# Identity built first on GpSimd, a 112-column last output piece, and newly searched orders and engines in a linear-attention and GEGLU block

## The chip, the cores and the metric

The kernel runs on one core of a Trainium2 chip, in one launch. The metric is device time in microseconds (us); the time before is the median of three runs, 190.91 us. TensorE is PE, its weight load PEld, VectorE DVE, ScalarE ACT, GpSimd POOL, and SyncE, which issues all DMAs, SP.

## The reference

```python
x = A_x                                   # [1, 2048, 448] bf16
h = x + _A_ref(_layernorm(x), A_wqkv, A_wo)
h2 = h + _B_ref(_layernorm(h), B_w_gate, B_w_up, B_w_down)

def _A_ref(x, wqkv, wo):                  # 16 heads of 28, no softmax
    q, k, v = split(x @ wqkv)             # wqkv [448, 1344]
    phi = lambda t: jnp.where(t > 0, t + 1, jnp.exp(t)) + 1e-6
    kv = einsum("bhsd,bhse->bhde", phi(k), v)
    z = einsum("bhsd->bhd", phi(k))
    num = einsum("bhqd,bhde->bhqe", phi(q), kv)
    den = einsum("bhqd,bhd->bhq", phi(q), z)[..., None] + 1e-6
    return merge_heads(num / den) @ wo    # wo [448, 448]

def _B_ref(x, w_gate, w_up, w_down):      # 448 -> 1792 -> 448
    return (gelu_tanh(x @ w_gate) * (x @ w_up)) @ w_down
```

## The kernel before

The 2048 rows are 16 tiles of 128 rows, numbered 0 to 15. Every piece of work is a named task with its engine, and the order in which each engine's tasks stand is a table of numbers in the source (`ORDERS`, five strings in the order PE, ACT, DVE, POOL, SP). A second table (`BANKS`) gives each PSUM tile one of the eight banks, and `ENGINE` names the engine of tasks that could run on more than one. Nothing is reordered when the kernel runs: an engine works through its string and waits on semaphores.

The tasks that the text speaks of, t being a tile:

- `warm` is ten matmuls of 512 columns on a tile of ones, whose result nobody reads; `ident` is the 128x128 identity, which POOL makes from the ones (L384).
- Layer norm 1: `ast`, `aag` on DVE (mean and variance, L423, L424), `aln`, `ars` on ACT (the root, by logarithm and exponential), `anm` (the negated mean), `norm` (L467 on DVE or L470 on POOL), `dup` (a copy of the last 64 columns, for odd tiles).
- `tr0` to `tr3` transpose tiles 0 to 3 on PE against the identity (L482 to L484) and `ev0` to `ev3` evict them; tiles from 4 on are transposed in pairs by a DMA, `xT5`, `xT7` and so on (L491).
- `ks0`, `ks1` are the k projections of the first two tiles (L524); `ka`, `kb` (L537) and `qa`, `qb` (L635) are the two halves of the k or q projection of a pair of tiles, `ka4` that of tiles 4 and 5. After k come `ek`, `cl`, `ph` (exponential, clamp, sum), after q `eq`, `cq`, `pq`.
- `g0a`, `g0b`, `g2a`, `g2b` with a tile's number add phi(k) times the normalised x into four PSUM banks (L561), four matmuls per tile in each of two groups of banks. Each such task is two matmuls that run side by side, one on the upper and one on the lower 64 rows of the array; `a` and `b` of one tile write the same two banks with the halves exchanged. The same holds for `ka`/`kb` and the other a/b pairs.
- Then `evg`, `zbm`, `evz`, `kvp`, `kz1`, `mm` fold v and wo into one matrix; `mul`, `den`, `rd`, `om`, `wo` divide by the denominator, project and add; layer norm 2 gives `hn` and its transposed tiles.
- `gua`/`gub` are the gate and up projections (L835, L838), `ge` the gelu on ACT (L861), `hm` the product on DVE (L863), `da`/`db` the down projection of a pair of tiles (L785), `down14`, `down15` those of the last two tiles alone (L799), `out` the residual sum on DVE (L805), `dout` the store (L807). The last tile is computed and stored in two pieces of columns.

All DMAs stand in the one queue of SP, in the order of its string.

```python
for t in self.order[ename]:            # emit(): one engine's string
    ...                                # waits on what t reads and overwrites
    ins = t.fn(eng)
```

Of the kernel before, what the change touches and what calls it, by code (L numbers as in the profile page):

```python
# [238 lines left out]
def bass_sequential_preLN__linear_attn_block__glu_gated_geglu__prompt_kernel(  # L239
# [34 lines left out]
    with es:  # L274
# [495 lines left out]
        p_op = []  # L770

        def b2_tile(t, kd):
            parts = [(0, D)] if t < T - 1 else [(0, D // 2), (D // 2, D)]
            pair = t < T - 2
            if pair and t % 2 == 0:
                p_op.clear()
# [162 lines left out]
```

## Time and profile before

| what | before |
|---|---|
| runs | 190.91, 190.93, 190.7 us |
| the profiled execution | 190.84 us, of which the span from first to last instruction is 189.1 us |
| granted PE clock | 1.000 |
| PE busy | 184.3 us (97%), 1940 matmuls |
| DVE, ACT, POOL busy | 117.3, 76.3, 69.1 us |

The profiled execution is 0.07 us under the median. Busy time of PE counts a matmul from its start to its modelled end; matmuls overlap, so the spacing of their starts tells the pace, and "mean ns of one" is longer than that spacing. In the timeline a row is a run of equal instructions: start, length to the end of the last, count, and in brackets the idle time before with what ended it.

### The profile page before, as it was taken

The page shows a single profiled execution, that of the slowest core. Times are in us where ns is not written, and L with a number is a line of the kernel's source. Part 1 is how long each engine was busy: PE and PEld are TensorE (multiplying, and loading weights), DVE is VectorE, ACT ScalarE, POOL GpSimd, SP SyncE. Part 2 cuts the span into 40 slices and gives each one's busy share as a digit, 9 for nine tenths or more (in the row PEclk, how much of TensorE's full clock was granted, in tenths as well). Part 3 has the DMA queues.
Part 4 walks back from the last instruction along what each step waited for, and adds up shares of the span by engine and source line. Part 5 has one row for each costly group of instructions (what it writes and reads, how often), then busy time and mean ns, then how long its engine had stood idle before and what let it go on. Part 6 is the DMA issues. An engine that isn't in the chain of part 4 may idle for free.

```text
span 189.1 us, 4840 instructions
## 1 busy us (share of the span) xinstructions
PE 184.3 (97%) x1940; PEld 105.8 (56%) x1940; DVE 117.3 (62%) x296; ACT 76.3 (40%) x210; POOL 69.1 (37%) x120
## 2 busy tenths in 40 slices
PE   7899999999999999999999999999999999999994
PEld 2344555544687886654444455445555666665643
DVE  7999966597998979368773438445534253344332
ACT  3789734688973432300343520043453223032200
POOL 1668732398889579910039500054000000000000
DMA  5898389806925372560003262002320000000204
GB/s 140 246 234 142 75 171 322 234 3 143 296 54 59 57 231 37 100 85 1 0 0 62 39 109 54 3 2 52 92 45 0 3 2 24 3 0 0 76 21 149
DMA packets 32694, 15.93 MB, mean 84 GB/s; under 512 B 21536, under 2 KB 32416, under 8 KB 32672
## 3 DMA queue, kind: packets, MB, share of 16 engines
q1 hardware_dynamic: 32672, 15.63, 36.1%
q8 instruction: 15, 0.25, 0.6%
q14 instruction: 7, 0.06, 0.1%
HBM read 8.37 MB, written 1.84 MB: 54 GB/s over the span
## 4 chain that ended last, share of the span: by engine, by line
PE 95%; DMA 1%; POOL 1%; DVE 1%; ACT 1%; issue 0%; POOLq 0%; DVEq 0%
PE ps L835 41%; PE ps L785 20%; PE ps L561 7%; PE ps L635 5%; PE ps L537 5%; PE ps L717 5%; PE ps L838 4%; PE ps L799 3%; DMA x_sb<-in_A_x_dram 1%; PE ps L524 1%; PE ps L706 1%; PE ps L618 1%; POOL xn L470 1%; PE ps L599 1%; DVE st L423 0%
## 5 line engine op out<-in xcount | busy, mean ns | idle before, releaser
L838 PE MATMUL ps<-hnT,wgu_sb 64*128 64x512 bf16 (+1 forms) x490 | 87.1, 333 | 0.0
L835 PE MATMUL ps<-hnT,wgu_sb 64*128 64x512 bf16 (+1 forms) x490 | 87.1, 333 | 0.0
L863 DVE TENSOR_TENSOR hh<-ps,gl 128x256 bf16<-128x256 f32 x112 | 42.5, 417 | 46.4 <-ACT gl L861 45.6
L861 ACT ACTIVATE gl<-ps 128x256 bf16<-128x256 f32 x112 | 36.0, 385 | 80.7 <-PE ps L838 38.7
L835 PEld LDWEIGHTS ps<-hnT,wgu_sb 64*128 64x128 bf16 x490 | 46.1, 94 | 32.4 <-issue 0.2
L838 PEld LDWEIGHTS ps<-hnT,wgu_sb 64*128 64x128 bf16 x490 | 45.9, 94 | 0.2
L785 PE MATMUL ps<-wd_sb,hh 64*128 64x448 bf16 x392 | 39.4, 349 | 0.0
L785 PEld LDWEIGHTS ps<-wd_sb,hh 64*128 64x128 bf16 x392 | 21.2, 94 | 15.8 <-issue 0.2
L680 POOL TENSOR_TENSOR o<-pq,rd 128x448 bf16<-128x448 bf16 x16 | 14.8, 943 | 20.4 <-DVE rd L677 20.4
L423 DVE BATCH_NORM_STATS2 st<-x_sb 128x6 f32<-128x448 bf16 x32 | 19.1, 613 | 0.5 <-DMA x_sb<-in_A_x_dram 0.4
L674 POOL TENSOR_TENSOR prod<-pq,zb 128x448 f32<-128x448 bf16 x16 | 16.3, 1034 | 4.2 <-DVE zb L270 4.2
L805 DVE TENSOR_TENSOR x_sb<-ps,x_sb 128x448 bf16<-128x448 f32 (+1 forms) x17 | 9.9, 590 | 8.9 <-PE ps L799 4.7
L561 PE MATMUL ps<-pk,xn 64*128 64x448 bf16 (+1 forms) x128 | 15.0, 350 | 0.1
L726 DVE TENSOR_TENSOR x_sb<-ps,x_sb 128x448 bf16<-128x448 f32 x16 | 9.4, 617 | 5.9 <-PE ps L717 5.0
L505 ACT ACTIVATE e<-ps 128x448 bf16<-128x448 f32 x20 | 10.1, 538 | 6.2 <-PE ps L537 5.4
L635 PE MATMUL ps<-wq_sb,xnT 64*128 64x448 bf16 x112 | 12.1, 350 | 0.0
L537 PE MATMUL ps<-wk_sb,xnT 64*128 64x448 bf16 x98 | 11.9, 350 | 0.2
L507 POOL TENSOR_SCALAR tm<-e 128x448 bf16<-128x448 bf16 x15 | 8.4, 563 | 8.3 <-ACT e L505 5.9
L429 POOL TENSOR_SCALAR nm<-mv 128x2 f32<-128x2 f32 (+1 forms) x13 | 2.9, 225 | 21.5 <-DVE mv L424 21.1
L717 PE MATMUL ps<-m_sb,oT 64*128 64x448 bf16 x98 | 10.7, 349 | 0.0
L512 DVE SCALAR_TENSOR_TENSOR pk<-ps,tm 128x448 bf16<-128x448 f32 x16 | 9.7, 619 | 1.0 <-ACT tm L503 0.3
L561 PEld LDWEIGHTS ps<-pk,xn 64*128 64x128 bf16 (+1 forms) x128 | 6.5, 97 | 6.6 <-PE ps L561 1.9
(84 smaller groups left out, 147.9 us busy)
## 6 DMA issues: line engine op xcount, KB each, us to landing
out_dram<-x_sb SPq DMA_DIRECT2D x15, 112.0 KB, 1.8
wd_sb<-in_B_w_down_dram SPq DMA_DIRECT2D x3, 448.0 KB, 6.5
wgu_sb<-in_B_w_up_dram SPq DMA_DIRECT2D x3, 384.0 KB, 6.9
wgu_sb<-in_B_w_gate_dram SPq DMA_DIRECT2D x3, 384.0 KB, 4.5
x_sb<-in_A_x_dram SPq DMA_DIRECT2D x2, 448.0 KB, 4.7
x_sb<-in_A_x_dram SPq DMA_DIRECT2D x4, 112.0 KB, 2.1
x_sb<-in_A_x_dram SPq DMA_DIRECT2D x2, 224.0 KB, 3.5
wo_sb<-in_A_wo_dram SPq DMA_DIRECT2D x1, 392.0 KB, 7.0
```

The lines of the kernel that those rows point to most:

```text
L423: op("dve", lambda e: e.bn_stats(st[:, t, :], src_ap()), [b_src], [b_st[t]], nm + "st%d" % t, 0.615, key)
L537: ins = e.matmul(ps[:, p_k[n].bank, 0:D], xnT[rows, t0 + n, k, :], wk_sb[rows, k, :], start=(k == 0 and not second), stop=(second and k == ...
L561: ins = e.matmul(ps[0:b - a, p_gx[cc].bank, 0:D], xnv(t, a, b)[rows], pk[rows, i, :], start=(t == 0 and not second), stop=(t == T - 1), sk ...
L635: ins = e.matmul(ps[:, p_q[n].bank, 0:D], xnT[rows, ts[n], k, :], wq_sb[rows, k, :], start=(k == 0 and not second), stop=(second and k == ...
L674: op(me, lambda e, ip=ip, p3=p3: e.tensor_tensor(prod[:, ip, :, 0:28], p3(), zb[:].rearrange("p (a e) -> p a e", e=28), ALU.mult), [b_pq[t ...
L680: return e.tensor_tensor(o2[:, so, n, :].rearrange("p (a e) -> p a e", e=28), p3(), rd[:, i, :].unsqueeze(2).to_broadcast([128, 16, 28]), ...
L717: ins = e.matmul(ps[:, p_h[n].bank, 0:D], oT2[rows, so, kk, :], m_sb[rows, kk, :], start=(k == 0 and not second), stop=(second and k == 2) ...
L785: ins = e.matmul(ps[:, p_d[n].bank, 0:D], hh[rows, j, u * 128:(u + 1) * 128], wd_sb[rows, j, :], start=(j == 0 and not second), stop=(j == ...
L835: e.matmul(ps[:, pa.bank, jj * N:(jj + 1) * N], wgu_sb[A_, wa + k if k < 3 else 3, jc], hnT[A_, k, c0:c0 + N], start=(k == 0 and jj == 0 a ...
L838: ins = e.matmul(ps[:, pb.bank, jj * N:(jj + 1) * N], wgu_sb[B_, wb + k if k < 3 else 3, jc], hnT[B_, k, c0:c0 + N], start=(k == 0 and jj ...
L861: G.add("act", lambda e, gi=gi, cs=cs, p_g=p_g: e.activation(gl[:, gi, cs], ps[:, p_g.bank, cs], AF.Gelu_apprx_tanh), r=[p_g], w=[b_gl[gi] ...
L863: op("dve", lambda e, dst=dst, gi=gi, cs=cs, p_u=p_u, rs_=rs_: e.tensor_tensor(dst, rs_(ps[:, p_u.bank, cs]), rs_(gl[:, gi, cs]), ALU.mult ...
```

## The change

The change replaces all of `ORDERS` and `BANKS` and the list `ENGINE`, and makes two edits in the code: the last tile's two pieces are 336 and 112 columns wide instead of 224 and 224, and a duration that only the planner reads is now a formula. All lines below the tables have moved down by one.

```diff
 ENGINE = (
-    "ev0:act anm1:act dup1:act dup3:pool norm4:dve dup5:pool dup9:pool cl2:act cl3:dve cl4:act cl5:act norm14:dve"
-    " norm15:dve dup15:pool cl7:act cl8:dve cl10:dve cl13:dve cl14:dve evz:dve evm1:act cq2:act cq4:act cq5:act cq6:act"
-    " cq7:act cq8:act cq13:act cq15:act evo1:dve evh0:dve evh1:act bnm2:act wrap3:pool wrap4:pool wrap5:pool wrap7:pool"
+    "anm0:act ev0:act ev1:act dup3:pool anm6:act dup7:pool anm8:act cl0:dve anm10:act cl2:act cl3:dve anm12:act cl4:act"
+    " norm15:dve dup15:dve cl6:dve cl7:act cl8:dve cl11:act cl13:dve cl14:dve evg0:act evg1:dve evm1:act cq4:act cq5:act"
+    " cq7:act cq8:act cq15:act evo1:dve evh0:dve evh1:act bnm2:act wrap2:pool bnm4:act wrap4:pool wrap5:pool wrap7:pool"
+    " bnm10:act bnm12:act"
 )
...
         def b2_tile(t, kd):
-            parts = [(0, D)] if t < T - 1 else [(0, D // 2), (D // 2, D)]
+            parts = [(0, D)] if t < T - 1 else [(0, 336), (336, D)]
...
-                   "out%d_%d" % (t, c0), 0.625 if c1 - c0 == D else 0.392, kd)
+                   "out%d_%d" % (t, c0), 0.16 + (c1 - c0) / 960.0, kd)
```

Of the order table the first entries of POOL show the manner of it (task numbers are those of the order in which the tasks are declared; 9 is `ones`, 10 `ident`, 11 `eps`, 46 `anm2`, 49 `norm2`):

```diff
-    "9 11 46 12 49 10 54 57 65 69 70 96 24 100 76 25 80 79 281 278 87 58 91 92 90 289 114 118 117 145 141 177 22 144 26 172"
+    "9 10 11 12 24 22 25 46 49 23 54 57 65 69 68 100 80 81 79 279 282 287 91 90 58 26 290 154 118 117 145 144 168 171 197"
```

The start of POOL's string before: `ones`, `eps`, `anm2`, `lnc`, `norm2`, `ident`, `anm3`, `norm3`.

```order
L383 MEMSET ones_bf 128x128
L386 MEMSET small 128x1
L429 ISA
L429 TENSOR_SCALAR nm<-mv 128x1
L387 MEMSET small 128x1
L470 TENSOR_SCALAR xn<-x_sb,nm,rs 128x448
L384 AFFINE_SELECT ident<-ones_bf 128x128
L429 TENSOR_SCALAR nm<-mv 128x1
L470 TENSOR_SCALAR xn<-x_sb,nm,rs 128x448
```

The same place now: `ones`, `ident`, four small constants, `mask_a`, `anm2`, `norm2`, then `powwarm` (L399), `anm3`, `norm3`.

```order
L384 MEMSET ones_bf 128x128
L385 ISA
L385 AFFINE_SELECT ident<-ones_bf 128x128
L387 MEMSET small 128x1
L388 MEMSET small 128x1
L400 MEMSET mones 112x4
L398 MEMSET small 128x2
L401 AFFINE_SELECT mtmp<-mones 112x4
L430 TENSOR_SCALAR nm<-mv 128x1
L471 TENSOR_SCALAR xn<-x_sb,nm,rs 128x448
L399 TENSOR_TENSOR small<-small 128x1
L430 TENSOR_SCALAR nm<-mv 128x1
```

The identity moved from behind `norm2` to the second place, and with it the ISA row (POOL's configuration, which the built program puts ahead of the first instruction that needs it); the one-element power that warms POOL (`powwarm`, before at L398 between later tasks) now stands between `norm2` and `anm3`. The first transposes on PE are `tr2`, `tr0`, `tr3`, `tr1` before and `tr2`, `tr0`, `tr1`, `tr3` now.

PE from `ks0` to the first matmuls of the g group before. The rows are `ks0` `ks1`; `ka2` `kb2`; `qa0` `qa2` `qb0` `qb2`; `ka4`; `g0a0`; `kb4`; and then `g0b0`, `g0a1`, `g0b1`, `g0a2` and the first matmul of `g2a0` in one row.

```order
L524 MATMUL ps<-wk_sb,xnT 128x448 x8
L537 MATMUL ps<-wk_sb,xnT 128x448 x14
L635 MATMUL ps<-wq_sb,xnT 128x448 x28
L537 MATMUL ps<-wk_sb,xnT 128x448 x8
L561 MATMUL ps<-pk,xn 128x448 x2
L537 MATMUL ps<-wk_sb,xnT 128x448 x6
L561 MATMUL ps<-pk,xn 128x448 x9
```

The same place now: `g0a0` and `g0b0` stand among the q halves (`qa0`; `g0a0`; `qb0` `qa2`; `g0b0`; `qb2`), then `ka4`, `g0a1`, `kb4`, `g0b1` and on.

```order
L525 MATMUL ps<-wk_sb,xnT 128x448 x8
L538 MATMUL ps<-wk_sb,xnT 128x448 x14
L636 MATMUL ps<-wq_sb,xnT 128x448 x8
L562 MATMUL ps<-pk,xn 128x448 x2
L636 MATMUL ps<-wq_sb,xnT 128x448 x14
L562 MATMUL ps<-pk,xn 128x448 x2
L636 MATMUL ps<-wq_sb,xnT 128x448 x6
L538 MATMUL ps<-wk_sb,xnT 128x448 x8
L562 MATMUL ps<-pk,xn 128x448 x2
L538 MATMUL ps<-wk_sb,xnT 128x448 x6
L562 MATMUL ps<-pk,xn 128x448 x3
```

Four matmuls moved ahead of `ka4`, and `kb4` now stands between `g0a1` and `g0b1`, which stood next to each other.

PE behind the single matmul `zbm` (L588) before: `g0b14`, `g0a15`, `g0b15` in one row, then `qa4`, `kvp`.

```order
L588 MATMUL ps<-gx,ones_bf 128x448
L561 MATMUL ps<-pk,xn 128x448 x6
L635 MATMUL ps<-wq_sb,xnT 128x448 x8
L599 MATMUL ps<-gx,wvt_sb 112x112 x4
L599 MATMUL ps<-gx,wv_sb 112x112 x12
```

The same place now: `g0b14`, `g0a15`; `qa4`; `g0b15`; `qb4`; `kvp`.

```order
L589 MATMUL ps<-gx,ones_bf 128x448
L562 MATMUL ps<-pk,xn 128x448 x4
L636 MATMUL ps<-wq_sb,xnT 128x448 x8
L562 MATMUL ps<-pk,xn 128x448 x2
L636 MATMUL ps<-wq_sb,xnT 128x448 x6
L600 MATMUL ps<-gx,wvt_sb 112x112 x4
L600 MATMUL ps<-gx,wv_sb 112x112 x12
```

`qa4` moved between `g0a15` and `g0b15`. In the rest of the program the gate, up and down tasks stand in another order too, without a new kind of row; at the end PE's last rows are 28 matmuls of `db12`, 14 of `down14` and 14 of the last piece in both.

75 rows, old and new, of tables (BANKS, ORDERS) are left out of this document.

## The prediction

> **What bounds the kernel now.** I read the page first, then busy time by stage, then PE's timeline where PE was not full. From the page:
>
> ```profile
> span 189.1 us, 4840 instructions
> PE 184.3 (97%) x1940; PEld 105.8 (56%) x1940; DVE 117.3 (62%) x296; ACT 76.3 (40%) x210; POOL 69.1 (37%) x120
> PE 95%; DMA 1%; POOL 1%; DVE 1%; ACT 1%; issue 0%; POOLq 0%; DVEq 0%
> ```
>
> PE is busy 97% of the span and makes up 95% of the chain that ended last. The stages (PE's busy time beside each stretch):
>
> ```profile
> 13.90:35.70 21.80, 21.73 (x223) 1.00 0.84 195
> 49.60:186.40 136.80, 136.80 (x1514) 1.00 0.24 50
> ```
>
> From 13.9 us on PE hardly pauses. A new order can win only ahead of 13.9, in short stalls inside the busy stretch, and after the last matmul; everywhere else it can only lose. PE's head:
>
> ```profile
> 5.53 0.34 PE L482 MATMUL ps<-ident,xn 128*128 128x128 bf16 x3 [0.86 <-POOL ident L384]
> 6.07 0.34 PE L482 MATMUL ps<-ident,xn 128*128 128x128 bf16 x3
> 6.65 0.34 PE L482 MATMUL ps<-ident,xn 128*128 128x128 bf16 x3
> 7.10 0.34 PE L482 MATMUL ps<-ident,xn 128*128 128x128 bf16 x3
> 7.56 2.00 PE L524 MATMUL ps<-wk_sb,xnT 128*128 128x448 bf16 x8
> 10.96 2.81 PE L635 MATMUL ps<-wq_sb,xnT 64*128 64x448 bf16 x28
> 13.91 0.93 PE L537 MATMUL ps<-wk_sb,xnT 64*128 64x448 bf16 x8
> ```
>
> These are tr2, tr0, tr3, tr1, ks0/ks1, the four q halves and ka4. One matmul of 448 columns lasts 0.35 and the next pair starts 0.19 later, so after the q halves (end 13.77) PE could have gone on at 13.77 - 0.35 + 0.19 = 13.61; ka4 came at 13.91: 0.30 idle.
>
> **The change, part by part.**
>
> *Identity first.* POOL's head, then DVE's, then ACT's row with ars1:
>
> ```profile
> 3.84 0.24 POOL L429 TENSOR_SCALAR nm<-mv 128x1 f32<-128x1 f32 x1 [2.81 <-DVE mv L424]
> 4.51 0.71 POOL L470 TENSOR_SCALAR xn<-x_sb,nm,rs 128x448 bf16<-128x448 bf16 x1 [0.40 <-ACT rs L436]
> 5.18 0.29 POOL L384 TENSOR_SCALAR_AFFINE_SELECT ident<-ones_bf 128x128 bf16<-128x128 bf16 x1
> 8.32 0.71 POOL L470 TENSOR_SCALAR xn<-x_sb,nm,rs 128x448 bf16<-128x448 bf16 x1 [0.41 <-ACT rs L436]
> 2.27 0.33 DVE L393 MEMSET xn<- 128x320 bf16 x1
> 5.64 0.36 DVE L467 TENSOR_SCALAR xn<-x_sb,mv,rs 128x448 bf16<-128x448 bf16 x1
> 5.92 0.62 DVE L423 BATCH_NORM_STATS2 st<-x_sb 128x6 f32<-128x448 bf16 x1
> 6.46 0.38 DVE L467 TENSOR_SCALAR xn<-x_sb,mv,rs 128x448 bf16<-128x448 bf16 x1
> 9.11 0.38 DVE L467 TENSOR_SCALAR xn<-x_sb,mv,rs 128x448 bf16<-128x448 bf16 x1
> 6.09 0.20 ACT L436 ACTIVATE rs<-ln 128x1 f32<-128x1 f32 x1
> ```
>
> The identity fits into POOL's 2.81 us of waiting, so tr2 waits for norm2 (4.51 + 0.71 = 5.22) and starts near 5.27, 0.26 earlier. Little of that lasts. tr0 hangs on norm0 (DVE 5.64), which comes about 0.09 earlier because its root now stands ahead of tile 3's: tr0 at 5.99. tr1 no longer stands behind tr3: norm1 comes at 6.4 (ars1 ends 6.29), tr1 at 6.81. But tile 3 loses: powwarm stands ahead of anm3 on POOL, and ars3 behind aln1 on ACT (about 6.14), so norm3 runs about 6.29 to 7.0. tr3 follows tr1 after 0.46 (6.65 to 7.10 gives 0.45) at 7.27, and ks0 comes 0.46 later at 7.73, where it was 7.56: **+0.17**. powwarm itself costs
>
> ```profile
> L398 POOL TENSOR_TENSOR small<-small x1: 575/575/575, 47.9 to 47.9; 128x1 f32<-128x1 f32 x1
> ```
>
> 0.58, which norm3 can bear up to tr1's end, 7.27.
>
> *g0a0 and g0b0 ahead of ka4.* Two pairs of matmuls, 2 x 0.19 = 0.38, go into the idle 0.30 and push ka4 to 13.61 + 0.17 + 0.38 = 14.16. Before, the same work would have been done at 13.91 + 0.38 = 14.29: **-0.13**, if ka4's data are there. They come by xT5:
>
> ```profile
> 9.52 1.33 SPq L491 DMA_TRANSPOSE xnT<-xn  x1
> DMA to landing us min/median/max: 2.8/3.1/4.6
> ```
>
> norm4 moved from DVE (9.11) to POOL behind norm5 (8.32, and 0.3 later now, because the memset of xn, 0.33, has moved from DVE's waiting time into its busy time ahead of aag4). So norm5 8.6 to 9.3, norm4 to 10.0, and xT5 is issued near 10.0 instead of 9.52. On SP's queue it still stands behind the x tiles 8 to 11 and ahead of 12 to 15. Before, it landed just ahead of 13.91, some 4.3 after its issue. With the same latency it is 0.5 later: ka4 at 14.4, work-equal +0.11. If the 448 KB transfer ahead of it sets the landing, nothing changes. Bounds -0.13 to +0.11; I take **-0.10**, nearer the first, since 4.3 against a median of 3.1 speaks for a wait behind that transfer. After ka4 the waits are close but covered: ph4, xT7 and ph6 come within 0.2 us of their use by the same reckoning.
>
> *Halves pulled apart.* g0b1 right behind g0a1, and g0b15 right behind g0a15, show a stall:
>
> ```profile
> 15.48 0.97 PE L561 MATMUL ps<-pk,xn 64*128 64x448 bf16 x6
> 35.58 0.98 PE L561 MATMUL ps<-pk,xn 64*128 64x448 bf16 x6
> 30.27 1.30 PE L561 MATMUL ps<-pk,xn 64*128 64x448 bf16 x12
> PEld ps L561 <- PE ps L561: 1.9, 5, 0.5
> ```
>
> Three pairs should take 2 x 0.19 + 0.36 = 0.74; the first two rows, which hold those neighbours, take 0.97 and 0.98. The third is a control without such neighbours: six pairs, 5 x 0.19 + 0.36 = 1.31, and it took 1.30. The waits name L561 waiting for itself. Both neighbours are parted now by work that exists anyway (kb4, qa4): 2 x 0.235 = **-0.47**. ka2/kb2 stay neighbours.
>
> *The tail.*
>
> ```profile
> 182.49 4.16 PE L799 MATMUL ps<-wd_sb,hh 128*128 128x448 bf16 x28
> 185.35 0.62 DVE L805 TENSOR_TENSOR x_sb<-ps,x_sb 128x448 bf16<-128x448 f32 x1 [1.59 <-PE ps L799]
> 186.76 0.39 DVE L805 TENSOR_TENSOR x_sb<-ps,x_sb 128x224 bf16<-128x224 f32 x1 [0.79 <-PE ps L799]
> 185.57 0.95 SPq L807 DMA_DIRECT2D out_dram<-x_sb  x2
> 187.18 0.33 SPq L807 DMA_DIRECT2D out_dram<-x_sb  x1
> L799 PE MATMUL ps<-wd_sb,hh 128*128 128x224 bf16 x28 | 3.0, 259 | 0.0
> 37.45 0.82 PE L599 MATMUL ps<-gx,wv_sb 128*112 128x112 bf16 x12
> L599 PE MATMUL ps<-gx,wv_sb x12: 215/215/257, 37.4 to 38.1; 128*112 128x112 bf16 x12
> L799 PEld LDWEIGHTS ps<-wd_sb,hh 128*128 128x128 bf16 x42 | 3.9, 98 | 2.0 <-issue 0.7
> ```
>
> The wider early piece delays down14 by 14 x 112 columns, 0.65 at 2.4 columns per ns (448 take 0.19). The narrow piece saves nearly as much: its 224-column forerunner steps by (4.16 - 14 x 0.189 - 0.26) / 13 = 0.096, and twelve matmuls of 112 columns took 0.82, the last of it 0.215, so (0.82 - 0.215) / 11 = 0.055 a step; 14 x (0.096 - 0.055) = 0.57. The last sum shrinks from 0.39 by half of (0.62 - 0.39) to 0.28. It would end at 187.15 + 0.08 - 0.11 = 187.12. But tile 14's sum now starts at 186.0 and ends at 186.62, and only then can its store be issued. Two issues in a row take 0.95, so the last one starts at 187.1 to 187.2, as before (187.18), and right behind another 112 KB store, which may cost it some 0.1 at landing. Ends -0.1 and +0.3; I take **+0.10**. Where the gain of the narrower sum goes is SP's queue.
>
> *The other 1700 matmuls and the engine moves.* The same matmuls of the same shapes, at PE's full rate: **0**, covered by 30% or more idle time on ACT, DVE and POOL. ACT gets evz and loses evg1, two relu clamps and exponentials in two forms. Following evg3, evz, kvp, kz1, mm and wo by hand with the rows' durations, the tightest is about 0.1 us ahead of its use.
>
> Sum: -0.10 - 0.47 + 0.10 = -0.47 from 190.84, so **190.4 us**. Against the median 190.91 that is -0.27%. About 0.2%, 0.38 us, is what a measurement of this kernel can tell from no change.
>
> **The rivals.**
>
> *Two late transfers.* xT5 at its late bound (+0.21 on the sum) and the last store at its own (+0.20): 190.8, no change. For it: both bounds rest on one row each. Against: each alone is not enough. 0.21.
>
> *The stalls aren't of neighbours.* If those 0.23 us came from something at these times rather than this order, they stay: 190.84 - 0.10 + 0.10 = 190.85. For it: two cases only; against: the control. 0.06.
>
> *The weight load paces the narrow piece.* Its 128x128 load lasts 98 ns in the row above. If loads did not overlap, each step is 98, not 55: 14 x 0.043 = 0.60 more, 191.0. Against: the steps of 55 in the L599 row, each with a load of its own. 0.05. [...]
>
> *A bank comes free too late among the gelu tasks (slower).* Before, PE never waited there. A hand-over is one gelu and one product:
>
> ```profile
> L863 DVE TENSOR_TENSOR hh<-ps,gl 128x256 bf16<-128x256 f32 x112 | 42.5, 417 | 46.4 <-ACT gl L861 45.6
> L861 ACT ACTIVATE gl<-ps 128x256 bf16<-128x256 f32 x112 | 36.0, 385 | 80.7 <-PE ps L838 38.7
> ```
>
> If a gate task finds its bank unread by one hand-over, PE waits 0.385 + 0.417 and two signals, about 0.9: 191.3. It decides from one whole lost hand-over on. Against: DVE and ACT are half idle there. 0.10.
>
> *POOL's configuration isn't free (slower).* The instruction ahead of ident sets POOL up; before, whatever that takes lay in the 2.81 us gap above. The row bounds it: anm2 started 0.09 after its data, so it is over by 3.84. Even that late, ident ends at 4.13, norm2 at 5.7, and tr0 and tr1 hold: under 0.1. It matters only if the cost grows with what follows: 2.5 us late gives 192.9. [...] 0.03.
>
> **How the numbers follow.** The forecast 0.48; more than that (190.0, head and tail both at their good bounds, -0.2) 0.07; the others as given. Faster 0.55, same 0.32, slower 0.13. The range takes in the good bounds (190.0) and the cases up to 191.0, and leaves out the two slower rivals and a little below: 190.0 to 191.05.
>
> **What would show it.** tr2 near 5.27 and ks0 near 7.73; ka4 at 14.15 to 14.4; no row of six matmuls at 0.97 around g0b1 and g0b15; PE's wait at L562 for itself smaller; the last store's issue at 187.2 less the gain. A PE wait over 0.3 between 14 and 186 us would make it wrong.

## The result, and the profile after

The changed kernel takes 193.15 us (median of 17 runs, 191.54 to 195.56); the kernel before, beside it, 191.02 us (17 runs, 190.7 to 192.65). The ratio is 1.0082, with a 95% interval of 1.0055 to 1.0109: slower, where 190.4 us and "faster" were forecast. The ratio leaves out the four runs of lowest clock, since they lie over 1.5% above the fastest, and still holds the eight at 0.991.

The runs fall into three heaps by the granted PE clock: five at 0.999 to 1.000 (191.54 to 192.35 us, median 191.92), eight at 0.991 (193.0 to 193.85), four at 0.982 (194.93 to 195.56). So there are two losses to find: about 0.8 us at full clock, and a clock that is not full in 12 of 17 runs. The profiled execution is one at full clock (191.54 us); it shows the first loss and cannot show the second.

The head of its page, and the two long stretches from the windows (us, PE busy, PEld, DVE, ACT, POOL, clock, DMA share, GB/s):

```profile
span 189.8 us, 4856 instructions
PE 185.1 (98%) x1940; PEld 105.1 (55%) x1940; DVE 116.6 (61%) x295; ACT 75.9 (40%) x216; POOL 70.2 (37%) x116
14.60:36.15 21.55, 21.55 (x223) 11.17 (x221) 15.96 (x39) 12.46 (x34) 10.39 (x20) 1.00 0.77 185
50.24:187.08 136.84, 136.84 (x1514) 81.97 (x1512) 75.95 (x199) 41.68 (x132) 40.29 (x60) 1.00 0.21 47
```

The long stretch from 50 us on is what it was: 136.84 us. The difference is in front of it. PE's head, from its timeline, and its longest waits:

```profile
1.05 4.45 PE L419 MATMUL ps<-ones_bf 128*128 128x512 bf16 x10 [1.05 <-POOL ones_bf L384]
5.29 0.53 PE L483 MATMUL ps<-ident,xn 128*128 128x128 bf16 x3
6.00 0.50 PE L483 MATMUL ps<-ident,xn 128*128 128x128 bf16 x3
7.17 0.34 PE L483 MATMUL ps<-ident,xn 128*128 128x128 bf16 x3 [0.43 <-DVE xn L468]
7.62 0.34 PE L483 MATMUL ps<-ident,xn 128*128 128x128 bf16 x3
8.07 1.03 PE L525 MATMUL ps<-wk_sb,xnT 128*128 128x448 bf16 x4
PE ps L754 <- ACT hn L743: 0.6, 1, 0.6
PE ps L483 <- DVE xn L468: 0.4, 1, 0.4
```

`tr2` stands at 5.29 as forecast, but `tr1` (7.17) waits for `norm1`, and `ks0` comes at 8.07 instead of 7.56. And there is a new wait of 0.6 us at L754, the transposes `trh1` and `trh0` of layer norm 2. Stage by stage, between starts of the same tasks:

| stage | before, us | after, us | difference |
|---|---|---|---|
| start to `ks0` | 7.56 | 8.07 | +0.51 |
| `ks0` to `trh1` | 41.14 | 40.59 | -0.55 |
| `trh1` to `trh0` | 0.45 | 1.14 | +0.69 |
| `trh0` to the last matmul | 137.24 | 137.28 | +0.04 |
| last matmul to the end | 2.73 | 2.75 | +0.02 |

The place of the +0.69, POOL and DVE of the kernel before:

```profile
47.85 0.57 POOL L398 TENSOR_TENSOR small<-small 128x1 f32<-128x1 f32 x1
48.40 1.03 POOL L674 TENSOR_TENSOR prod<-pq,zb 128x448 f32<-128x448 bf16 x1
48.05 0.15 DVE L732 SCALAR_TENSOR_TENSOR small<-mv,rs 128x1 f32<-128x1 f32 x1
```

and POOL, DVE, ACT and PE of the changed kernel:

```profile
47.81 1.03 POOL L675 TENSOR_TENSOR prod<-pq,zb 128x448 f32<-128x448 bf16 x1
48.01 0.85 DVE L733 SCALAR_TENSOR_TENSOR small<-mv,rs 128x1 f32<-128x1 f32 x1
48.90 0.76 ACT L743 ACTIVATE hn<-x_sb,small,rs 128x448 bf16<-128x448 bf16 x1 [0.63 <-DVE small L733]
49.80 0.33 PE L754 MATMUL ps<-ident,hn 128*128 128x128 bf16 x3 [0.62 <-ACT hn L743]
```

Before, `powwarm` (L398) stood on POOL between `cq11` and the product `mul6` (L674), and the one-column operation `bnr0` on DVE ran beside it in 0.15 us. With `powwarm` gone to the head, `mul6` starts 0.6 us earlier; `bnr0` now starts inside it, takes 0.85 us and ends with it (48.86 and 48.84). ACT's `normh0` and PE's `trh0` stand behind it.

The same picture in the head: DVE's `norm1` and POOL's `norm3` run at once, and `norm1`, 0.38 us before, takes 0.73.

```profile
6.39 0.73 DVE L468 TENSOR_SCALAR xn<-x_sb,mv,rs 128x448 bf16<-128x448 bf16 x1
6.27 0.72 POOL L471 TENSOR_SCALAR xn<-x_sb,nm,rs 128x448 bf16<-128x448 bf16 x1 [0.46 <-ACT rs L437]
```

The two places where halves were pulled apart, PEld's wait at L562 for PE, and the tail:

```profile
16.16 1.36 PE L562 MATMUL ps<-pk,xn 64*128 64x448 bf16 x12
35.76 0.55 PE L562 MATMUL ps<-pk,xn 64*128 64x448 bf16 x4
PEld ps L562 <- PE ps L562: 1.8, 6, 0.3
183.78 3.51 PE L800 MATMUL ps<-wd_sb,hh 128*128 128x448 bf16 x28
186.64 1.03 DVE L806 TENSOR_TENSOR x_sb<-ps,x_sb 128x448 bf16<-128x448 f32 x2 [1.18 <-PE ps L800]
187.32 0.96 SPq L808 DMA_DIRECT2D out_dram<-x_sb  x2
```

No row of six matmuls takes 0.97 any more. The tail's last sum ends at 187.67 and the second of the last two stores is issued right behind the first.

### The profile page after: what moved, and what is told of

Same layout as the page of the kernel before. It is cut to its first block, busy times and chain, and to the rows that moved or that the text cites. A ratio compares the mean times of both kernels' runs of the same rounds, so it can differ in the third digit from the quotient of the medians.

```text
span 189.8 us, 4856 instructions
## 1 busy us (share of the span) xinstructions
PE 185.1 (98%) x1940; PEld 105.1 (55%) x1940; DVE 116.6 (61%) x295; ACT 75.9 (40%) x216; POOL 70.2 (37%) x116
## 4 chain that ended last, share of the span: by engine, by line
PE 93%; DVE 3%; DMA 1%; issue 1%; ACT 0%; SPq 0%; DVEq 0%
PE ps L836 41%; PE ps L786 20%; PE ps L562 7%; PE ps L538 5%; PE ps L718 5%; PE ps L636 4%; PE ps L839 4%; PE ps L800 3%; DVE st L424 1%; DMA x_sb<-in_A_x_dram 1%; PE ps L707 1%; PE ps L525 1%; PE ps L619 1%; DVE xn L468 1%; PE ps L600 1%
## 5 line engine op out<-in xcount | busy, mean ns | idle before, releaser
L864 DVE TENSOR_TENSOR hh<-ps,gl 128x256 bf16<-128x256 f32 x112 | 41.7, 415 | 43.6 <-ACT gl L862 42.8
L681 POOL TENSOR_TENSOR o<-pq,rd 128x448 bf16<-128x448 bf16 x16 | 14.9, 944 | 13.8 <-DVE rd L678 13.7
L562 PE MATMUL ps<-pk,xn 64*128 64x448 bf16 (+1 forms) x128 | 15.5, 351 | 0.0
L806 DVE TENSOR_TENSOR x_sb<-ps,x_sb 128x448 bf16<-128x448 f32 (+2 forms) x17 | 9.8, 589 | 8.8 <-PE ps L786 7.5
L506 ACT ACTIVATE e<-ps 128x448 bf16<-128x448 f32 x23 | 11.8, 537 | 5.7 <-PE ps L538 4.7
L508 POOL TENSOR_SCALAR tm<-e 128x448 bf16<-128x448 bf16 x17 | 9.5, 563 | 12.3 <-ACT e L506 10.6
L636 PE MATMUL ps<-wq_sb,xnT 64*128 64x448 bf16 x112 | 12.7, 350 | 0.0
L746 POOL TENSOR_SCALAR hn<-x_sb,nm,rs 128x448 bf16<-128x448 bf16 x14 | 10.0, 717 | 5.9 <-ACT nm L430 5.1
L471 POOL TENSOR_SCALAR xn<-x_sb,nm,rs 128x448 bf16<-128x448 bf16 x13 | 9.5, 733 | 3.0 <-ACT rs L437 2.9
```

The source lines that it names most:

```text
L562: ins = e.matmul(ps[0:b - a, p_gx[cc].bank, 0:D], xnv(t, a, b)[rows], pk[rows, i, :], start=(t == 0 and not second), stop=(t == T - 1), sk ...
L636: ins = e.matmul(ps[:, p_q[n].bank, 0:D], xnT[rows, ts[n], k, :], wq_sb[rows, k, :], start=(k == 0 and not second), stop=(second and k == ...
L681: return e.tensor_tensor(o2[:, so, n, :].rearrange("p (a e) -> p a e", e=28), p3(), rd[:, i, :].unsqueeze(2).to_broadcast([128, 16, 28]), ...
L864: op("dve", lambda e, dst=dst, gi=gi, cs=cs, p_u=p_u, rs_=rs_: e.tensor_tensor(dst, rs_(ps[:, p_u.bank, cs]), rs_(gl[:, gi, cs]), ALU.mult ...
```

## The experiments

"Full clock" below means runs granted 0.999 or 1.000. The kernel before was run beside the experiments 132 times: 29 runs (22%) were granted 0.991 or less, and the other 103 have a median of 191.12 us. Each experiment has 12 runs, e6 six.

### The late trh0: powwarm and bnr0

`e2_before_powwarm_head` moves `powwarm` alone (23, with the memset that it reads, 22; the constant 12 comes one place earlier), in POOL's string of the kernel before. 439 is `mul6`:

```diff
-9 11 46 12 49 10 54 57 ... 177 22 144 ... 321 23 439
+9 11 12 22 23 46 49 10 54 57 ... 177 144 ... 321 439
```

> The kernel before, with powwarm alone moved (and the memset it reads): it runs in POOL's idle 2.8 us at the very start, so that mul6 follows cq11 at once near 47.8 us. Nothing else in the head moves. Theory A: bnr0 takes about 0.85 us instead of 0.14, trh0 is 0.65 us late, and the best runs take about 191.5. Theory M for the clock: more than half of the runs also drop to 0.991 or 0.982, median 192.5 to 193.5. Theory H: all runs stay at 1.0, median 191.5. Rival: nothing changes, 190.9, and the stall of the changed kernel came from its other moves.

Measured: 191.90 at full clock (9 of 12 runs), the kernel before beside it 191.10; ratio 1.0057, 1.0034 to 1.0081 (this ratio, like the others below, also holds runs at 0.991). POOL, DVE and PE:

```profile
48.12 1.02 POOL L676 TENSOR_TENSOR prod<-pq,zb 128x448 f32<-128x448 bf16 x1
48.31 0.85 DVE L734 SCALAR_TENSOR_TENSOR small<-mv,rs 128x1 f32<-128x1 f32 x1
50.02 0.34 PE L755 MATMUL ps<-ident,hn 128*128 128x128 bf16 x3 [0.53 <-ACT hn L744]
```

One instruction of 0.58 us, moved into a gap where it costs nothing, makes the kernel 0.8 us slower at full clock, by the stall that the changed kernel shows. Three of 12 runs lost clock, about the share of the kernel before: theory M, that this stall lowers the clock, falls.

`e1_powwarm_back` puts `powwarm` back ahead of `mul6` (440 there) in the changed kernel:

```diff
-... 46 49 23 54 57 ... 322 440
+... 46 49 54 57 ... 322 23 440
```

> The changed kernel with one POOL instruction put back: powwarm (0.58 us) stands just ahead of mul6 again instead of in the head. Theory A (the late trh0): in the changed kernel bnr0 on DVE took 0.85 us instead of 0.14 because mul6 ran on POOL beside it, and trh0 came 0.65 us late; with powwarm ahead of mul6, bnr0 takes 0.14 again and PE's wait of 0.6 us at the transposes near 49 us is gone. In the head norm3 ends about 0.6 us earlier, no longer beside norm1, which takes 0.38 instead of 0.72: ks0 at about 7.7. Together the best runs come to 190.6 to 190.9. Theory M for the clock (12 of 17 runs of the changed kernel were granted 0.991 or 0.982 of full clock, and were 1.5 or 3.2 us longer): the 1.5 us near 49 us in which PE only transposes and waits lowers the clock, so without the wait nearly all runs are at 1.0 and the median is 190.6 to 191.0. Theory H: the clock is lost to the head, because full rate is granted later or taken back there; then more than half of the runs stay at 0.991 or below and the median is about 192.2. Rival to A: bnr0's 0.85 us has another cause, and trh0 stays 0.65 us late.

```profile
49.25 0.58 POOL L401 TENSOR_TENSOR small<-small 128x1 f32<-128x1 f32 x1
49.44 0.15 DVE L735 SCALAR_TENSOR_TENSOR small<-mv,rs 128x1 f32<-128x1 f32 x1
49.80 1.03 POOL L677 TENSOR_TENSOR prod<-pq,zb 128x448 f32<-128x448 bf16 x1
```

Measured: `bnr0` 0.15 us beside `powwarm`, no wait at the transposes, 191.02 at full clock against 191.92 of the changed kernel (the profiled execution runs 1.4 us late here, for a reason that the part on the clock gives). But 5 of 12 runs lost clock, so the median of all is 191.48. In the head `norm3` did not come earlier (6.21; it waits for `ars3`, not for `powwarm`), and `norm1` still took 0.77: that part of the expectation was wrong.

`e4_bnr_one_tensor` leaves every order of the changed kernel as it is and only writes `bnr0` and `bnr1` in another form:

```diff
-scalar_tensor_tensor(nr2[:, t:t + 1], mv2[:, t, 0:1], -1.0, rs2[:, t:t + 1], ALU.mult, ALU.mult)
+tensor_scalar(nr2[:, t:t + 1], mv2[:, t, 0:1], rs2[:, t:t + 1], -1.0, ALU.mult, ALU.mult)
```

> The changed kernel with bnr0 and bnr1 written as a tensor_scalar with one tensor input (the mean) and the reciprocal deviation as a pointer scalar, instead of an operation on two tensors; the same product. Theory P (port): a DVE instruction that reads two tensors from SBUF can't run beside POOL's two-tensor product mul6, one that reads a single tensor can: bnr0 takes 0.15 to 0.2 us although mul6 runs beside it, trh0's wait of 0.6 us goes, best runs about 190.9. [...] For the clock, theory M expects 1.0 in nearly all runs if the wait goes, theory H more than half under 0.995 either way, since the head is untouched.

```profile
47.77 1.03 POOL L675 TENSOR_TENSOR prod<-pq,zb 128x448 f32<-128x448 bf16 x1
47.98 0.20 DVE L733 TENSOR_SCALAR small<-mv,rs 128x1 f32<-128x1 f32 x1
```

`bnr0` runs beside `mul6` in 0.20 us, `trh0` follows `trh1` by 0.49, and the median at full clock is 191.18. So POOL being busy does not by itself hold `bnr0`: beside a `mul6` of 1.03 us it took 0.85 us with two tensors read and 0.20 with one. The new form is also another kind of instruction, but the old kind is not always held: `pq`, of that kind with one of its two tensors in PSUM, runs beside `mul6` (48.40 to 49.43) in the kernel before, and two of them take 1.15 us, 1.12 just ahead of it:

```profile
47.01 1.12 DVE L644 SCALAR_TENSOR_TENSOR pq<-ps,tm 128x448 bf16<-128x448 f32 x2
48.11 1.15 DVE L644 SCALAR_TENSOR_TENSOR pq<-ps,tm 128x448 bf16<-128x448 f32 x2
```

For `norm1` the count of tensors explains nothing: it reads one, and took 0.73 us beside `norm3` in the changed kernel and 0.40 apart from it in e9. What makes an instruction wait for POOL's the traces do not show.

### The clock: what PE does between the warm matmuls and ks0

e4's head is that of the changed kernel, and 6 of its 12 runs lost clock (were granted 0.991 or less). The profiled run of `e1_powwarm_back` happened to be one of them (192.31 us, clock 0.991). Its windows:

```profile
0.83:4.24 3.41, 3.19 (x8) 1.16 (x9) 2.46 (x5) 1.72 (x3) 1.04 (x8) 1.00 0.62 146
4.24:7.66 3.42, 2.28 (x20) 1.04 (x19) 3.42 (x11) 2.20 (x9) 1.64 (x3) 1.00 0.92 252
7.66:11.07 3.41, 3.41 (x12) 0.88 (x11) 2.08 (x10) 2.15 (x6) 1.64 (x3) 0.50 0.89 273
11.07:14.48 3.41, 3.34 (x34) 1.44 (x35) 1.85 (x4) 2.16 (x7) 1.20 (x2) 1.00 0.68 122
```

Full clock was granted at 4.24 us, while the warm matmuls ran; taken back at 7.66, 0.5 us ahead of `ks0` (8.19); and granted again at 11.07: half clock for exactly one stretch of 3.41 us. (The 1.00 of the first row is no grant, since the view counts the time ahead of the first one as full: the warm matmuls start 0.427 us apart there and 0.216 apart behind the grant.) In e11, too, the clock changed only at such steps (below). What parts the stretches in these traces is not a gap (the longest here is 0.7 us; e13 below kept the clock across 1.9 us) and not PE's busy time (67% here, 44% in e13), but the share of a stretch that PE streams. Busy time overstates that: a 128-column transpose of the kernel before counts 0.22 to 0.24 us, and the next one starts 0.06 us behind it. Counting each matmul as its columns at 2.4 columns per ns (1.2 at half clock; 512 columns in 0.216 and 0.427 us above), matmuls side by side once, the stretch 4.24 to 7.66 is streamed 37% of the time.

`e5_filler` adds two matmuls to e4, in PE's 0.7 us of idle time ahead of `tr1`; nothing reads their result:

```diff
                         ins = e.matmul(tv[64:128, 3, :], xnv(t, 384, D), ident[:], start=True, stop=True)
+                        if t == 0:
+                            free = [q for q in G.tiles if q.name == "tp1"][0].bank
+                            for _ in range(2):
+                                e.matmul(ps[:, free, 0:512]..., ones_bf[:], ones_bf[:]..., start=True, stop=True)
```

> The kernel with bnr0 on one tensor (e4_bnr_one_tensor), and two extra matmuls of 512 columns on the ones tile right behind tr0, into a bank that nothing holds yet; their result is not used. They fill PE's idle 0.7 us ahead of tr1 with 0.43 us of work (0.85 at half clock). Theory H, with the traces' numbers: the clock is granted anew in stretches of 3.41 us; a stretch in which PE was busy 67% was followed by half clock (4.24 to 7.66 us in the trace of e1_powwarm_back), stretches with 74, 75 and 80% were followed by full clock (e2, e3, e4). The stretches that fall between the end of the warm matmuls and ks0 are lifted from about 62 to 67% up to 75% or more, so at most 2 of 12 runs are granted less than 0.995 (6 of 12 in e4), the median is 190.9 to 191.3. Rival: the lost clock has nothing to do with how busy PE is in the head (it comes from the chip at random, or from a later stage); then 4 or more of 12 runs stay under 0.995, median about 191.8.

Measured: 0 of 12 runs lost clock (6 of 12 in e4; beside it 4 of 12 in e8, which has e4's head, and 9 of 29 in the kernel before); median 191.40, all runs between 190.96 and 191.94. The shares of 67 to 80% in the expectation are of PE's busy time; by streamed columns they are 37 to 46%.

`e6_before_warm8` takes two of the ten warm matmuls away from the kernel before, `e12_before_warm12` adds two:

```diff
-    WARM = cfg.get("warm", 10)
+    WARM = cfg.get("warm", 8)      # e12: 12
```

> The kernel before, with 8 warm matmuls instead of 10 and nothing else changed. PE's useful work is the same, and the warm matmuls end 0.43 to 0.85 us earlier, so PE waits that much longer ahead of tr2. Theory H: the stretches ahead of ks0 fall to 56 to 64% busy, so more than half of the runs are granted 0.991 or less (4 of 35 in the kernel before), median 192.3 to 193.5; the best runs stay near 190.8. Rival (the lost clock has nothing to do with PE's busy share in the head): at most 2 of 12 runs under 0.995, median 190.9 to 191.2.

> The kernel before, with 12 warm matmuls instead of 10 and nothing else changed: PE computes 0.43 to 0.85 us more that nobody uses. Theory H, with PE's streaming shares: half clock followed a stretch of 3.41 us with 37% and full clock stretches with 44% and more, and the kernel before lies at 44 to 45%, just above; two more matmuls lift it to 50% or more. So 0 or 1 of 12 runs are under 0.995 (13 of 64 in the kernel before so far), and the median is 191.0 to 191.3. Rival: the lost clock isn't in the head; then 2 to 3 of 12 stay under 0.995.

e6: 193.42 us, all six runs between 193.27 and 194.03, although five of them show a granted clock of 1.000. Its trace has the first grant at 12.69 us, and its eight matmuls of `ks0` and `ks1` take from 8.25 to 11.21, 2.96 us instead of the 1.65 of the kernel before: the mean counts the clock from the first grant on, and a grant that comes late is not in it. So e6's expected price came, but in another way than expected: full clock was not taken back, it came at least two stretches late. e12: 0 of 12 runs lost clock, median 191.06, highest 191.84; the kernel before beside it 191.34, 9 of 29 lost.

`e11_before_parted_first` (its order is in the next part) had its profile taken at clock 0.982, 194.43 us; its windows, and `norm0` on DVE:

```profile
0.50:3.91 3.41, 2.86 (x7) 1.01 (x8) 2.56 (x7) 1.40 (x2) 0.30 (x3) 1.00 0.55 130
3.91:7.33 3.42, 1.97 (x17) 0.89 (x15) 3.19 (x9) 2.10 (x10) 2.10 (x6) 1.00 0.79 206
7.33:10.74 3.41, 2.63 (x14) 0.92 (x12) 2.47 (x7) 1.56 (x4) 1.18 (x3) 0.50 0.98 299
10.74:14.15 3.41, 3.41 (x13) 0.88 (x12) 1.52 (x6) 1.41 (x4) 1.26 (x4) 0.50 0.66 127
14.15:17.57 3.42, 3.35 (x35) 1.67 (x36) 2.37 (x5) 2.31 (x6) 1.68 (x4) 1.00 0.36 122
5.96 0.73 DVE L469 TENSOR_SCALAR xn<-x_sb,mv,rs 128x448 bf16<-128x448 bf16 x1
```

Two stretches at half clock: the heap at 0.982. Here DVE waited 0.2 us for each of two loads, and that made `norm0` meet POOL's `norm` (0.73 us instead of 0.36), and PE streamed 36% of 3.91 to 7.33; the next stretch, at half clock, reached 54% and half clock stayed; behind the one after, with 92%, full clock came back. The stretches of the head in which the share comes nearest to a change, and those of the runs compared here (the trace of the kernel before has no record of the clock; its stretches are read off the pace of the warm matmuls). They are laid in steps of 3.41 us from the first grant of each run, forward and back; that the steps hold also where the clock does not change is an estimate from e1 and e11:

| run, stretch | streamed | clock in the stretch behind it |
|---|---|---|
| e11, 3.91 to 7.33 | 36% | taken back |
| e1, 4.24 to 7.66 | 37% | taken back |
| e13, 11.91 to 15.32 | 39% | stays full |
| e10, 5.06 to 8.48 | 42% | stays full |
| before, 3.65 to 7.06; e2, 3.68 to 7.10 | 44% | stays full |
| e4, 5.69 to 9.11 | 46% | stays full |
| e12, 4.56 to 7.98 | 50% | stays full |
| e5, 5.65 to 9.07 | 55% | stays full |
| e11, 7.33 to 10.74 | 54% | half stays half |
| after, -0.07 to 3.35; e6, 2.45 to 5.87 | 67% | half stays half |
| e6, 5.87 to 9.28 | 69% | half stays half |
| before, 0.24 to 3.65; e2, 0.27 to 3.68 | 76 and 77% | raised to full |

In these traces, then, half clock stayed behind stretches of up to 69% and full clock followed 76% and more; full clock was taken back behind 36 and 37% and kept behind 39% and more. Each of these sides rests on one or two stretches, and no run shows what sets them. Without the columns of the transposes the stretches would not part so: e10's has 17% and kept the clock, e11's 20% and lost it. The kernel before lies at 44% in its profiled run, not far above 37%. In the changed kernel `tr1` and `ks0` come 0.5 us later, so a stretch that starts around 4 us holds one transpose fewer, and where the stretches fall is different in each run (the first grant came at 3.65 us in the kernel before, 4.24 in e1, 6.76 in the changed kernel). An estimate from the two profiled traces, with the warm matmuls at half clock up to the grant and everything else as it was recorded: in the changed kernel every stretch that starts between 3.6 and 4.8 us streams 35 to 38%, in the kernel before none that starts between 3.6 and 7.0 streams less than 42%. Where the load of wk comes late (the traces of e2 and e3) the kernel before, too, goes under 38% by this estimate, for starts from 4.4 to 5.0 and to 5.7 us. Kernels with the changed head and ten warm matmuls (after, e1, e4, e8) lost clock in 27 of 53 runs, those with 12 warm matmuls (e10, e12, e13, e14) in 0 of 48.

### The terms of the sum

`e3_before_ident_first`, the identity alone (POOL's string of the kernel before):

```diff
-9 11 46 12 49 10 54
+9 10 11 46 12 49 54
```

> The kernel before, with the identity alone made first on POOL. tr2 at 5.27 instead of 5.53; tile 3 no later than before, so ks0 at 7.4 to 7.56 and the time 190.7 to 190.9. Theory H for the clock in its form that the earlier transposes change when full rate comes: clocks under 0.995 in more than a third of the runs. Theory M: clocks at 1.0 as in the kernel before.

Measured: 191.34 at full clock (191.10 beside it), no gain; 2 of 12 lost clock. `tr2` started at 5.22, but `ks0` at 8.36, since it waited 0.79 us for the load of wk. That load's landing sets `ks0` in e2 (8.13), e7 (7.83), e10 (8.45), e12 (7.93) and e13 (7.94) too: the 7.56 of the kernel before was an early one.

`e9_norm1_apart` mends the head of e4: the root of tile 1 ahead of that of tile 3, and `norm1` ahead of tile 5's statistics.

```diff
-ACT ... 31 32 55 38 56 39 51     DVE ... 37 33 63 40 64
+ACT ... 31 32 38 39 55 56 51     DVE ... 37 33 40 63 64
```

> The kernel with bnr0 on one tensor (e4_bnr_one_tensor), with the head's order mended: on ACT aln1 and ars1 stand ahead of aln3 and ars3, on DVE norm1 stands ahead of the statistics of tile 5. So norm1 (DVE) runs from about 6.1 and norm3 (POOL) from about 6.45, one after the other. Theory P: norm1 took 0.68 to 0.77 us in the changed kernel and its variants because norm3 ran on POOL beside it, and takes about 0.38 now; tr1 starts near 6.6 instead of 7.13, tr3 near 7.2 instead of 7.6. ks0 then comes at about 7.65, or with the landing of wk's load, which was 7.4 to 8.3 in the traces; median at full clock 190.7 to 191.0 (e4 191.2). Theory H: PE's streaming share ahead of ks0 rises from 37 to 46% to about 48%, and at most 3 of 12 runs are under 0.995. Rival to P: norm1 takes 0.7 also by itself; then tr1 comes near 6.95. Rival to the gain: the weights' landing alone sets ks0, and nothing is gained.

```profile
6.21 0.40 DVE L470 TENSOR_SCALAR xn<-x_sb,mv,rs 128x448 bf16<-128x448 bf16 x1 [0.39 <-ACT rs L439]
6.72 0.72 POOL L473 TENSOR_SCALAR xn<-x_sb,nm,rs 128x448 bf16<-128x448 bf16 x1 [0.79 <-ACT rs L439]
144.26 0.37 PE L838 MATMUL ps<-hnT,wgu_sb 64*128 64x512 bf16 x1 [0.45 <-issue]
```

Apart, `norm1` takes 0.40, `tr1` starts at 6.67, and 1 of 12 runs lost clock. But `norm3` came later than expected, `ks0` at 7.94, and the median at full clock is 191.37, 0.2 over e4's. Part of that is the third row, a stall at 143.4 us in which PE waits for nothing that the profile shows: a step of 0.82 us between two matmuls. The usual step there is 0.18. It stands in e5 (0.66), e8 (0.65) and e10 (0.49) too and is small in e4 (0.30), never in the nine profiles of the kernel before and its variants; e1 and the changed kernel itself were profiled without it. Its cause stays open.

`e7_before_parted` and `e11_before_parted_first` pull halves apart in PE's string of the kernel before:

```diff
-104 106 108 129 103 131 105 ... 248 250 252 291 262
+104 106 103 108 129 131 105 ... 248 250 291 252 262     e7
+104 106 103 108 129 105 131 ... 248 250 252 291 262     e11
```

> The kernel before with two PE moves alone: g2a0 between g0a1 and g0b1, and qa4 between g0a15 and g0b15. By the prediction's step each parting takes 0.235 us: the rows of six matmuls of 0.97 and 0.98 us near 15.5 and 35.6 go, and the runs at full clock take 0.47 us less, a median of 190.6 beside 191.1. Rival: the time isn't in the neighbours but moves to the next pair, or is given back at the next wait; then 191.1, same as before.

> The kernel before with the first partings alone: g2a0 between g0a1 and g0b1, and g2b0 between g0a2 and g0b2, which e7_before_parted had made neighbours (its trace has a step of 409 ns there, while the step of 415 ns at g0a1/g0b1 fell to 319). No g0b stands right behind its g0a near 15 to 17 us. By the prediction's step the two stalls there (0.32 us each, with the 0.09 of a pair taken off) are gone, no step over 300 ns between 15 and 17 us, and ka4 to g0a3 takes 0.2 to 0.3 us less than before. Rival: the stall belongs to this place and moves on to another pair. The clock as in the kernel before: 1 to 5 of 12 runs under 0.995.

e7: 191.61 at full clock (7 of 12 runs), slower than the kernel before beside it (191.25). The step of 415 ns behind `g0a15` became 186, so the stall is one of these neighbours. But the other parting made new neighbours, `g0a2` and `g0b2`, and a step of 409 ns appeared there. And `g0b15` now came after `qa4`, so its bank was evicted later and PE waited:

```profile
PE ps L601 <- DVE gx L272: 0.5, 1, 0.5
```

e11: 191.01 at full clock (9 of 12 runs), 191.15 beside it. In e14, which has the same order, the step at `g0a1` fell only from 415 to 320 ns: `g2a0`, put in between, starts at 16.12 right behind `pq0` (16.07), whose bank it takes. No gain that can be measured.

`e8_half_tail` is e4 with pieces of 224 and 224 columns:

```diff
-[(0, 336), (336, D)]
+[(0, D // 2), (D // 2, D)]
```

> The kernel with bnr0 on one tensor (e4_bnr_one_tensor) with the last tile in pieces of 224 and 224 columns, as before the change. By the prediction's step the changed tail costs 0.10 us (ends -0.1 and +0.3), so the stretch from the last tile's first matmul to the end is 0.1 us shorter here than in e4. Rival: the tail gains or loses nothing (within 0.05). For the clock, theory H expects the same as for e4, 4 or more of 12 runs under 0.995, since the head is untouched.

From the start of the hundredth matmul from the end to the end of the span e8 takes 13.81 us and e4 13.87: the changed tail costs 0.06. Four of 12 runs lost clock.

### Both faults mended, and what is left

`e10_after_both_mended` is e4 with 12 warm matmuls.

> The changed kernel with bnr0 on one tensor (e4_bnr_one_tensor) and 12 warm matmuls instead of 10. Theory: with both faults mended the rest of the change is worth its terms in the traces, +0.4 to 0.5 in the head, -0.55 between 9 and 37 us, 0 in the tail: 190.9 to 191.2, within 0.2% of the kernel before at full clock; 0 or 1 of 12 runs under 0.995. Rival 1: the prediction's -0.47 holds by itself, 190.5 to 190.8. Rival 2: a stall near 143.5 us belongs to the changed order; then part of the runs is 0.5 us longer and the median 191.3 to 191.6.

Measured: 0 of 12 runs lost clock, median 191.20 (190.93 to 191.74); the kernel before beside it 190.97 at full clock, so 0.2 us longer by the medians; the ratio is 0.9987, 0.9952 to 1.0021, with the runs of the kernel before at 0.991 in it. The rest of the change gains nothing that can be measured. Its trace has `ks0` at 8.45, behind the load of wk:

```profile
8.45 2.00 PE L525 MATMUL ps<-wk_sb,xnT 128*128 128x448 bf16 x8 [0.36 <-DMA wk_sb<-in_A_wqkv_dram]
```

`e13_before_mended` put three parts into the kernel before: 12 warm matmuls, `g0a0` and `g0b0` ahead of `ka4`, and the partings.

```diff
-122 275 283 276 284 148 102 149 104 106 108 129 103 131 105 107 133 109 130 135 156 132 134 174 136
+122 275 102 276 283 104 284 148 106 149 108 103 129 105 107 131 109 130 133 132 134 135 156 174 136
```

> The version that the runs so far point to: the kernel before with three parts taken together. (1) 12 warm matmuls, as in e12_before_warm12. (2) g0a0 and g0b0 ahead of ka4, in PE's order of the changed kernel: they fill the 0.39 us that ka4's data are late by. (3) no g0b right behind the g0a of its tile near 15 to 17 us. powwarm stays ahead of mul6, the head's order and the tail stay as they were. Expected from the traces: (2) 0.1 to 0.3 us less, (3) 0.25 us less, so the trace shows ka4 to g0b3 0.4 to 0.5 us shorter than before in PE's loss, no wait over 0.3 us at the transposes near 49 us, and at most 1 of 12 runs under 0.995. Median 190.6 to 190.9, beside 191.1 to 191.4 of the kernel before. Rival: as in e7_before_parted, what is won early is given back at a wait for DVE near 37 us, and the median is 191.0 to 191.1, that of the warm matmuls alone.

A miss: 193.4 us. PE waits 1.9 us at the early `g0a0`:

```profile
14.18 0.36 PE L563 MATMUL ps<-pk,xn 64*128 64x448 bf16 x2 [1.91 <-DVE pk L514]
```

In the bank table of the kernel before the second of the two banks that `g0a0` adds into is that of `ka2`, free only after `ph2`; the changed kernel's table gives it that of `ks0`. The order of PE can't be copied without its banks. `e14_parted_warm12` leaves that part out (e11 with 12 warm matmuls).

> The kernel before with the first partings (e11_before_parted_first) and 12 warm matmuls (e12_before_warm12), nothing else. Theory: the partings are worth 0.25 to 0.3 us at full clock and 12 warm matmuls keep the clock: median 190.7 to 190.9, 0 or 1 of 12 runs under 0.995, no step over 300 ns between 15 and 17.5 us. Rival: the partings are given back later, 191.0 to 191.1 as in e12_before_warm12.

Measured: 0 of 12 runs lost clock, median 191.02, 190.64 to 191.44; the kernel before beside it 191.03 over all its runs, 190.58 to 193.45; ratio 0.9984, 0.9953 to 1.0014. It is not faster than the kernel before at full clock (190.97); what it has, like e12, is that no run loses clock: its highest run is 191.44, and over all experiments a run in five of the kernel before took over 192.5.

## Why the prediction was wrong

**The step that failed** is the term for the other 1700 matmuls and the engine moves: "The same matmuls of the same shapes, at PE's full rate: 0". It failed in both halves, the moves and the full rate. The price of `powwarm` was looked for only at its new place ("0.58, which norm3 can bear"), and there it does cost nothing (e1: without it `norm3` is no earlier). At its old place it kept `mul6` off `bnr0`, and taking it away costs 0.69 us in the trace and 0.7 to 0.9 by the medians at full clock (e2, e1, e4). The prediction had named the row that would refute it, "A PE wait over 0.3 between 14 and 186 us"; it came, at 49 us.

**The other half**, "at PE's full rate", missed a case that none of the rivals held: that the head takes the full clock back. One execution at clock 1.00 was taken for all. The traces of before had the means: the timeline shows ten warm matmuls and then 2.9 us with only the 20 short matmuls of the transposes. It is shown for e1 and e11 that the clock is lost there, and that filling this place ends it (0 of 60 runs with fillers or 12 warm matmuls); the changed kernel itself was not profiled while it lost clock, and for it the place is an estimate from its trace at full clock. Of the 2.1 us between the medians about 0.8 is `bnr0` and 1.2 the clock.

**Identity first** (+0.17 up to `ks0`): `tr2` at 5.29 and no cost of POOL's configuration, as forecast: `ident` started at 1.07, right behind `ones` (0.79 to 0.99), so no run shows the 2.5 us of the rival on it. `tr0` stood at 6.00. But `norm1` beside `norm3` took 0.73 instead of 0.38, so `tr1` came at 7.17 (6.81 forecast) and `ks0` at 8.07 (7.73): +0.51. And with the load of wk, for which `ks0` waited until 7.8 to 8.5 in six traces and 9.3 in that of e11, an earlier head could not have been worth much. The prediction had both, `norm1` at 6.4 and `norm3` from 6.29 to 7.0, and let them run side by side at no cost.

**g0a0 and g0b0 ahead of ka4** (-0.27 in itself, -0.10 with the head): `ka4` came at 14.60, outside the forecast 14.15 to 14.4; without the 0.34 that `ks0` was late it would be 14.26, inside. From `ks0` to `ka4` the work-equal gain is 6.35 - (6.53 - 0.38) = 0.20. The choice of the nearer bound was right:

```profile
10.55 1.34 SPq L492 DMA_TRANSPOSE xnT<-xn  x1
DMA to landing us min/median/max: 3.2/3.2/3.2
```

`xT5` was issued 1.03 us later than before and landed at the same time, 13.8 (9.52 + 4.3 before, 10.55 + 3.2 now). It was not the only thing that `ka4` waited for: in the kernel before `ph3` on DVE ended at 13.75, too. What was not seen: the idle 0.30 ahead of `ka4` was also a cushion. In the kernel before and its variants `ka4` came at 13.91, 13.99, 14.05 and 14.18 for `ks0` at 7.56, 7.93, 8.00 and 8.13, so up to 0.3 us of a late head were swallowed there. Once the gap is filled, every delay of the head counts in full.

**Halves pulled apart** (-0.47): right in the trace, while in the time of whole runs no experiment shows it (e7 and e11 above). Both steps of 415 ns are gone in the changed kernel (225 and 186 ns there), and e7 shows the stall following a new pair of neighbours. PEld's own wait at that line, though, fell only from 1.9 to 1.8 us: it is shared out over more, shorter waits. From `ka4` to `trh1` -0.35 arrives, the two moved pairs taken off (34.79 - 34.06 - 0.38).

**The tail** (+0.10, ends -0.1 and +0.3): +0.06. The step of the narrow piece is 0.049 us with weight loads of 98 ns, so the load does not pace it, as the trace's 55 ns had said. The store was issued at 187.82; the forecast of 187.2 less the gain falls with the delay before it. The store's 28 KB took 1.6 us from issue to landing, the last 56 KB of the kernel before 1.5.

**The sum.** 0.51 - 0.55 + 0.69 + 0.04 + 0.02 = +0.71 in the profiled run, where -0.47 was forecast: of the 1.18 between them 0.34 lies in the head, 0.69 at `trh0`, 0.12 in the halves. No rival named either of the first two. Two slips of the working changed nothing: the good bounds add up to 190.14, not 190.0, and with POOL's configuration at its latest the rows put the end of `norm2` at 5.5, not 5.7.

## What to carry to other kernels

When an instruction is moved, look at both places: at the old one list what ran beside it, and what will start earlier and run beside whom now; an instruction with no reader there may still be what keeps two others apart (`powwarm` here, 0.58 us long and worth 0.8 us in e2). The clock granted to the warm matmuls was not kept here: granted at 4.24 us in e1, it was taken back at 7.66. So count the columns that PE streams in every stretch (3.41 us in these traces) until the steady stage, and read the granted clock of all runs, with the time of the first grant (12.69 us in e6, at a mean clock of 1.000), before trusting one profile. A gap just behind a stage whose end varies can be a cushion, like the 0.30 us ahead of `ka4`; filling it turns the variation into time.

## What the hardware showed that was not expected

- `bnr0`, a DVE operation of one column on two SBUF tensors, started while POOL formed the product `mul6`, took 0.85 us instead of 0.15 and ended with it (48.86 and 48.84 in after, 49.16 and 49.14 in e2). With one tensor input it took 0.20 (e4). A DVE normalisation of 128x448 that started just behind the same on POOL took 0.68 to 0.77 us (0.73 in after, 0.77 in e1, 0.68 in e4, 0.73 in e11) instead of 0.36 to 0.40, and ended 0.12 to 0.14 us after POOL's. Where DVE's started first (`norm0` at 5.64 and `norm3` at 5.84 in the kernel before), it kept its 0.36, and POOL's took 0.75 instead of 0.71.
- The clock was taken back behind stretches of 3.41 us streamed 36% (e11) and 37% (e1), without any gap over 0.8 us, and kept behind 39% (e13) and more; it was not raised behind 67 and 69% (e6) and raised behind 76% (before). Neither PE's busy time (58 and 67% where the clock was lost, 44% where e13 kept it) nor the length of the gaps (e13 kept it across 1.9 us) parts these stretches.
- The mean granted clock did not hold the time ahead of the first grant: e6's runs took 193.4 us, five of six at 1.000, and its trace has the first grant at 12.69 us.
- In four of the six profiles of the changed kernel's descendants PE lost 0.3 to 0.6 us in one step (0.49 to 0.82 us instead of 0.18) near 143.5 us, with nothing to wait for in the profile. Open.
